# VectorE's score arrays hold three banks in place of two: wider shift passes in an attention and convolution kernel

## The chip, the cores and the metric

One core of a Trainium2 chip (trn2) runs the whole kernel. The metric is the device time of an execution in microseconds (us). The kernel before takes 719.72 us, the median of three runs (719.65 to 720.16). The core's engines work side by side, each through its own list of instructions, and wait for one another by semaphores: TensorE (PE, matmuls; PEld is its loading of weights), VectorE (DVE), ScalarE (ACT), GpSimd (POOL) and SyncE (SP). DMAs are issued from SP, POOL and ACT.

## The reference

Two independent blocks, whose results stand side by side in the output:

```python
# A: attention, S = 2048, D = 512, 32 heads of 16
qkv = x @ wqkv
scores = einsum("bhqd,bhkd->bhqk", q, k) * 16 ** -0.5
o = einsum("bhqk,bhkd->bhqd", softmax(scores), v)
a = o.reshape(B, S, D) @ wo
# B: a short and a long causal convolution, gated
kv = (k convolved with the 4 taps of shift_k) * v
y  = (kv convolved with ssm_k over all 2048 steps) + kv * ssm_D
b = q * y
out = concatenate([a, b], axis=-1)
```

All inputs are bf16. Nearly all of the time goes to A: 32 heads of 2048 x 2048 scores, each of which needs an exponential.

## The kernel before

**How the work is tiled.** The scores are cut into 2048 blocks of 128 keys by 512 queries of one head (512 columns in each of 128 partitions, one bank of PSUM). 64 blocks that belong together, 16 key tiles by four heads, are a group; 32 groups follow one another. Four blocks whose heads lie in different row groups can be multiplied side by side by PE (`qk_mm`, L910).

**Two engines make the exponentials.** ACT takes two or three banks at once with its exponential (`emit_exp`, L935: 128x1024 or 128x1536) and writes bf16 into a ring PT of 13 places. DVE takes one block at a time and makes the exponential without a table, in `exp_on_dve`: an addition with a floor (L1019) writes the score, scaled so that the bit pattern of the 16-bit result, read as a number, is about its power of two. Three more copies of this pattern, shifted by added integers, correct it: PV multiplies the values by all four terms with different weights (the first with VA, three with the scaled copies VS). The copies are made by two "shift passes" over bf16 data in SBUF:
- the near pass (L1029) writes one shifted copy of the first term;
- the far pass (L1036) writes two more from the first two, so it is twice as wide, and goes into a second array.

The arrays are RST, `R_ARR` of them, each with room for two terms of a set of blocks. A set is opened in the first free array by its first block (`take_array`); it is shifted when it holds its two blocks, or earlier as it is when the planner marks it "alone" (a group is being closed, or DVE has nothing else). The array of the first two terms is given back when these terms are multiplied for all blocks and the far pass has read it; the array of the far terms when those are multiplied (`give_back`). `R_LIN` limits how many sets may have their first array out at a time, and `dve_block` hands DVE no new set while no array is free.

**What sets the order.** All instruction lists are written by a planner that runs as the kernel is built. It goes step by step (T), gives each engine a clock of its own (`pe.t`, `dve.t`, `act.t`) and adds a price per instruction. At each step it emits the scores for ACT, perhaps a block for DVE (`dve_block`), terms to multiply (`pv_step`, L1128), and pieces of the rest: projections, the convolution (L1379, with weights WR read back from DRAM in 256 loads of 528 KB), output products, and filler matmuls that keep PE busy in gaps (`warm_up`, L1584). Ready shift passes wait in a list `flow` and are put where DVE has room, behind anything that empties a PSUM bank (`urgent`). `pv_step` multiplies terms when all four row groups have one, up to three levels at a time, and closes a group when all of its blocks are out.

A table, `POLICY`, changes the planner's thresholds as blocks go by (its first numbers count blocks). A class `Tensor` models that PE gets its instructions in stretches of 256, by loads that stand behind other DMAs: `FETCH` and `LOADED` say when the next stretch lands, and `release` holds back loads of WR that would delay it.

**The price list of the shift passes**, by the number of banks, as the planner sees it (time on the engine, time behind what it waits for):

```python
V512 = (0.60, 0.726)
FOUR = {1: (0.2, 0.326), 2: (0.333, 0.459), 4: (0.6, 0.726)}
```

A set of n blocks pays `FOUR[n]` for the near and `FOUR[2 * n]` for the far pass.

Of the kernel before, what the change touches and what calls it, by code (L numbers as in the profile page):

```python
# [88 lines left out]
N_TAIL = 9  # L89
MOST_OP = 3  # L90
OVER_OP = 0.1
R_ARR = 8
R_LIN = 5
LIN_D = 0.3
EVEN = 0.85
MOST_D = 3
# [52 lines left out]
WAIT = 3.0  # L149
LATE = 0.3  # L150
V512 = (0.60, 0.726)
FOUR = {1: (0.2, 0.326), 2: (0.333, 0.459), 4: (0.6, 0.726)}
TWO = {1: (0.333, 0.459), 2: (0.6, 0.726)}
SAME = 0.012
SWITCH = 0.105
# [3 lines left out]
BLOCK = 256  # L159
WORD0 = 65  # L160
FETCH = 3.3
SPAN = 6.0
QUIET = 6.0
LOADED = 1.6
WR_KB = 330
NEED = 10.0
FILL = 0.054


POLICY = (  # L170
    (0, {"DELAY": 3, "EVEN_MORE": 4, "FIRST": 2, "HALF": 0.35, "HURRY": 2, "JOIN": 0.15, "JOIN_D": 0.5, "LAGS": 16, "LATE": 0.3, "LATE_D": 0.4, "LEAD": 2, "LIN_D": 0.3, "LOW": 6.0, "LOW_2": 2.0, "LOW_A": 9.0, "LOW_L": 0.0, "MARGIN": 0.35, "MARGIN_D": 0.1, "MARGIN_P": 0.1, "MIN_L": 1, "NOW": 10, "OPEN": 40, "OVER_C": 0.1, "PRESS": 0, "PRIOR": 1, "R_LIN": 5, "SAFE": 1.0, "SOON": 0.3, "SOON_P": -0.1, "S_FX": 0.55, "TURN": 0.0}),
    (0, {"OVER_C": 0.05, "MIN_L": 2, "LIN_D": 0.0, "SAFE": 2.0}),
    (65, {"DELAY": 2, "JOIN": 0.25}),
    (194, {"LOW_2": 3.0}),
    (256, {"JOIN_D": 0.6, "EVEN_MORE": 6, "MARGIN_P": -0.3}),
    (320, {"LOW_2": 2.0, "JOIN_D": 0.5, "OVER_C": 0.1, "DELAY": 3, "EVEN_MORE": 4, "JOIN": 0.15, "MARGIN_P": 0.1, "MIN_L": 1, "LIN_D": 0.3, "SAFE": 1.0}),
    (384, {"JOIN": 0.25}),
    (448, {"PRESS": 20, "NOW": 6, "LOW": 5.5}),
    (514, {"MARGIN_P": 0.0, "OPEN": 30}),
    (578, {"LOW_2": 3.0, "PRESS": 0, "JOIN": 0.05, "MARGIN_P": 0.1, "NOW": 10, "OPEN": 40, "LOW": 6.0}),  # L180
    (640, {"PRIOR": 0, "HALF": 0.5}),
    (704, {"LOW_A": 2, "FIRST": 1}),
    (769, {"LOW_A": 9.0, "LOW_2": 2.0, "MARGIN": 0.32, "FIRST": 2, "PRIOR": 1, "JOIN": 0.15, "LEAD": 6}),
    (834, {"MARGIN": 0.35, "SOON_P": 0.1, "TURN": 0.2, "HALF": 0.35, "LEAD": 2, "SAFE": 2.0}),
    (899, {"LOW_2": 3.0, "LOW_L": 1, "MARGIN": 0.3, "R_LIN": 6, "SOON_P": -0.1, "TURN": 0.0, "SAFE": 1.0}),
    (961, {"HURRY": 0}),
    (1025, {"PRESS": 10}),
    (1090, {"LOW_2": 2.0, "LOW_L": 0.0, "LAGS": 10, "R_LIN": 5, "PRESS": 0, "HURRY": 2}),
    (1154, {"OVER_C": 0.0, "JOIN": 0.25}),
    (1218, {"MARGIN": 0.35, "OVER_C": 0.1, "LAGS": 8, "EVEN_MORE": 2, "JOIN": 0.15}),  # L190
    (1282, {"LOW_A": 5, "MARGIN_D": 0.0}),
    (1344, {"OVER_C": 0.15, "FIRST": 3, "LOW": 4.5, "SAFE": 2.0}),
    (1408, {"SOON": 0.2}),
    (1473, {"JOIN_D": 0.4, "OVER_C": 0.0}),
    (1537, {"JOIN": 0.05}),
    (1600, {"LOW_A": 2, "JOIN_D": 0.5, "MARGIN_D": 0.2, "OVER_C": 0.1, "LAGS": 16, "FIRST": 2, "EVEN_MORE": 4, "S_FX": 0.45, "JOIN": 0.15, "SOON": 0.3, "LOW": 6.0, "SAFE": 1.0}),
    (1665, {"JOIN_D": 0.7, "MARGIN": 0.3, "S_FX": 0.5, "LIN_D": 0.0}),
    (1729, {"LOW_A": 9.0, "JOIN_D": 0.5, "MARGIN_D": 0.1, "MARGIN": 0.35, "SOON_P": -0.2, "S_FX": 0.55, "LATE": 0.2, "TURN": 0.2, "LEAD": 6, "LIN_D": 0.3}),
    (1794, {"LAGS": 8, "DELAY": 4}),
    (1858, {"HURRY": 6, "JOIN": 0.05}),  # L200
    (1922, {"LAGS": 16, "HURRY": 2, "DELAY": 3, "SOON_P": -0.1, "LATE": 0.3, "JOIN": 0.15, "TURN": 0.0, "LEAD": 2, "LATE_D": 0.5}),
    (1985, {"LATE_D": 0.4}),
)


# [73 lines left out]
class Tensor(Eng):  # L279
# [32 lines left out]
    stalls = []  # L312

    def fetch(self, cross):
        end = max([b for a, b in self.loads[-12:] if a <= cross + 0.4], default=0.0)
        return max(cross + FETCH, end + LOADED)

    def spare(self):
# [15 lines left out]
def bass_concat_heads__mha_block__ssm_conv_h3__prompt_kernel(  # L334
# [25 lines left out]
    def sb(name, shape, dt=BF16):  # L360
# [24 lines left out]
    IDN = sb("IDN", [128, 128])  # L385
    IDP = sb("IDP", [128, 128])
    SHK = sb("SHK", [128, 4, 4])
    RST = sb("RST", [128, R_ARR, 2, 2, QB])
    VS = sb("VS", [128, 3, KT // 2, VROW])
    ZW = sb("ZW", [128, 32])  # L390
    JNK = sb("JNK", [128, 2], FP32)
# [12 lines left out]
    DG = OTF[:, 12 * QB + 2 * LEFT:16 * QB + 2 * LEFT].rearrange("p (c m d) -> p c m d", c=4, m=4)  # L404
    KZN = [OTF[:, 4 * QB:4 * QB + 2 * S].rearrange("p (c s) -> p c s", c=2),
           QNF[:, 0:2 * S].rearrange("p (c s) -> p c s", c=2)]
    XN = RST[:, R_ARR - 1, 0, :, :]
    PS = enter(nc.psum_tensor("PS", [128, 8, 512], FP32))


# [552 lines left out]
    def dve_block(T, n_act, aside=True):  # L963
        if T < T_DVE or aside and busy() or len(queue) < LAST_BLKS + 3 * TAIL_GAP + 4:
            return None
        if aside and conv_wants(T) and (state["go"] or conv_due() < T - PRESS):
            return None
        if aside and side[0] == "d" and (near(T, CLOSE) if T >= N_OPEN else early and early[0][0] <= T + 1):
            return None
        j = len(pairs) - 1  # L970
        j += not pairs or len(pairs[j]["h"]) == 2 or pairs[j]["alone"]
        if j == len(pairs) and (not arr_free or len([st for st in pairs[-8:] if 0 not in st["gone"]]) >= R_LIN or at(*arr_free[first_array()]) > pe.t + LIN_D):
            return None
        if todo() > BACKLOG:
            return None
        def pick_row(of, most):
            mine = [b for b in of if sub(b) == sub(of[0])][:most + EVEN_MORE]
            mine = [b for b in mine if even(b)]
            if not mine:
                return None  # L980
            there = [blk(b)[2] for b in on_dve if sub(b) == sub(of[0])]
            return min(mine, key=lambda b: there.count(blk(b)[2]))
        x = sub(queue[min(n_act, len(queue) - 1)])
        left = len([b for b in queue if sub(b) == x])
        if ends() + SAFE <= act.t + RATE * (left - n_act) + 1.3:
            return pick_row(queue, LOOK) if sub(queue[0]) == x else pick_row(queue[n_act:], 4)
        if x == subs[-1]:
            return None
        x = subs[subs.index(x) + 1]
        ahead = [b for b in queue if sub(b) == x]  # L990
        if len(ahead) < size[x] - AHEAD + 1 or x[0] not in h_q or (OF[x[0]], 0) not in h_k:
            return None
        return pick_row(ahead, 4)
# [11 lines left out]

    def give_back(st):
        for i in range(2):
            if i not in st["gone"] and min(st["n"][2 * i:2 * i + 2]) == len(st["h"]) and (len(st["h"]) == 2 or st["alone"]) and st["s"][1] is not None:
                st["gone"].add(i)
                arr_free[st["a"][i]] = (max(st["pv"][2 * i:2 * i + 2], key=lambda h: h[1]),) + ((st["s"][1],) if i == 0 else ())  # L1010

    def exp_on_dve(b, bank, h):
        if not pairs or len(pairs[-1]["h"]) == 2 or pairs[-1]["alone"]:
            a, dep = take_array()
            pairs.append({"h": [], "b": [], "alone": False, "a": [a, None], "s": [None, None], "dep": dep, "n": [0] * 4, "pv": [None] * 4, "gone": set()})
        j, half, st = len(pairs) - 1, len(pairs[-1]["h"]), pairs[-1]
# [6 lines left out]
        n = half + 1  # L1023

        def both(x, i0, i1):
            return x[:, i0:i1, 0:n, :].rearrange("p b a n -> p (b a n)") if n == 2 else x[:, i0:i1, 0, :]

        def near(us):
            st["s"][0] = dve.op(lambda e: e.tensor_scalar(both(lin, 1, 2).bitcast(U16), both(lin, 0, 1).bitcast(U16), SHIFTS[0], None, ALU.add),  # L1029
# [7 lines left out]
                                [st["h"][-1], st["s"][0], *dep], us=us)  # L1037
            give_back(st)

        begin = lambda: n == 2 or st["alone"]  # L1040
        if half == 0:
            st["f"] = [[]]
            flow.extend(st["f"])
# [117 lines left out]
    def pv_step(T):  # L1161
# [6 lines left out]
        for x in sorted({sub(b) for b in acts + dves}):  # L1168
# [7 lines left out]
            close = all(i in chunk_of for i in own) and T >= max(chunk_of[i] for i in own) + 2  # L1176
            if close and T < max(chunk_of[i] for i in own) + 2 + DELAY and n < NL and not any(p in pt_used for p in pt_next()):
                for b in d:
                    if len(pairs[on_dve[b][0]]["h"]) < MANY:
                        pairs[on_dve[b][0]]["alone"] = True  # L1180
                close = all(all_terms(b) is not None and at(all_terms(b)) <= pe.t + SOON_P for b in d)
            if close:
                for b in d:
                    while all_terms(b) is None:
                        k = dve.n
                        if len(pairs[on_dve[b][0]]["h"]) == 1:
                            pairs[on_dve[b][0]]["alone"] = True
                        if pick() is None:
                            early = next(y for y in d if all_terms(y) is not None and y in dves)
                            emit_pv([[(early, t)] for t in list(terms[early])], T)  # L1190
                            continue
                        advance(pick()[0] + MORE + 0.01)
                        assert dve.n > k
# [162 lines left out]
    def load_qn(i, deps):  # L1356
        for x in range(2):
            c0 = 256 * i + 128 * x
            h_qn[i] = dma(pool, d_q[0], QN[64 * x:64 * x + 64, :, :], q2[:, c0:c0 + 128].rearrange("(b i) d -> i b d", i=64),
                          deps if x == 0 else (), kb=930)  # L1360

    def conv_place(qd, g, rows):
        dst = PS[32 * g:32 * g + rows, BGB, :]
# [269 lines left out]
    while T < end[0] + 3:  # L1633
# [12 lines left out]
        advance(pe.t)  # L1646
        if LATE_D:
            late_block(T)
        if pairs and len(pairs[-1]["h"]) == 1 and not pairs[-1]["alone"] and dve.t < pe.t - ALONE and pick() is None:
            pairs[-1]["alone"] = True  # L1650
            advance(pe.t)
        emit_bg(T)
# [77 lines left out]
```

## Time and profile before

| | us |
|---|---|
| median of three runs | 719.72 |
| the profiled execution | 722.91 |
| its span | 721.1 |
| ACT busy | 703.4 (98%) |
| DVE busy | 691.3 (96%) |
| PE busy | 683.2 (95%) |
| POOL busy | 96.5 (13%) |

The profile shows one execution: from the span to the execution's own time there are 1.8 us outside of what is recorded. A group's row names its line, engine and operation, output and input with their shapes, its count, its busy time in all and the mean duration of one in ns; then the time its engine was idle just before, and the engine and line that ended most of it. Durations of neighbours on one engine can overlap, so the distance between two starts is shorter than a duration. The chain is the work that ended last, followed back from the end. PE's granted clock is given in shares of full speed.

### The profile page before, as it was taken

The numbers are of one execution on the slowest core, as the hardware profiler recorded it, in microseconds if no ns is written. First come the engines' busy times: TensorE is split into PE (matmuls) and PEld (weight loads), VectorE is DVE, ScalarE is ACT, GpSimd is POOL, SyncE is SP. The second block draws the span as 40 slices with busy tenths as digits, with TensorE's granted clock in tenths as the row PEclk, the third lists the DMA queues.
The fourth block names the chain that finished last, engine by engine and source line by source line (L and its number), as shares of the span: only waits on it lengthen the run. The fifth ranks groups of instructions, "written<-read, shape, count | busy, mean of one in ns | idle before, by whom it ended". The sixth has DMA issues, their size and how long they took to land.

```text
span 721.1 us, 25543 instructions
## 1 busy us (share of the span) xinstructions
PE 683.2 (95%) x11264; PEld 275.0 (38%) x11264; DVE 691.3 (96%) x1313; ACT 703.4 (98%) x646; POOL 96.5 (13%) x161
## 2 busy tenths in 40 slices
PE   9999999999899999999999999999999999999988
PEld 4334334334334434434333334333333333332244
DVE  5999999999799999999999999999999999999994
ACT  7999999999799999999999999999999999999997
POOL 5200311020020201002041020100202030211001
PEclk9999999999899999999999999999999999999999
DMA  9988644778857877588987578988885874713001
GB/s 229 289 215 270 141 168 140 258 254 299 269 204 277 292 269 264 161 306 294 332 258 217 184 247 313 338 288 307 295 318 189 310 281 163 288 57 59 16 17 32
DMA packets 83045, 164.23 MB, mean 228 GB/s; under 512 B 41232, under 2 KB 47256, under 8 KB 82680
## 3 DMA queue, kind: packets, MB, share of 16 engines
q1 hardware_dynamic: 75880, 153.61, 62.4%
q0 software_dynamic: 5856, 8.66, 4.9%
q8 instruction: 90, 1.47, 0.8%
q10 hardware_dynamic: 1200, 0.33, 0.2%
q14 instruction: 19, 0.16, 0.1%
HBM read 149.17 MB, written 8.54 MB: 219 GB/s over the span
## 4 chain that ended last, share of the span: by engine, by line
ACT 49%; DVE 32%; PE 18%; issue 1%
ACT PT L935 49%; DVE RST L1019 15%; DVE RST L1036 7%; PE PS L1128 7%; PE PS L910 6%; DVE RST L1029 4%; PE PS L1379 2%; DVE YB L1395 1%; DVE DT L1220 1%; PE PS L1294 1%; DVE KV L651 1%; PE PS L583 1%; DVE VA L666 1%; DVE KTo L640 1%; DVE VS L1060 0%
## 5 line engine op out<-in xcount | busy, mean ns | idle before, releaser
L935 ACT ACTIVATE PT<-PS 128x1024 bf16<-128x1024 f32 (+1 forms) x640 | 700.5, 1266 | 8.7 <-PE PS L910 7.8
L1019 DVE TENSOR_SCALAR RST<-PS 128x512 uint16<-128x512 f32 x513 | 342.6, 679 | 4.7 <-PE PS L910 4.0
L910 PE MATMUL PS<-QT,KTo 32*128 32x512 bf16 (+2 forms) x2248 | 257.6, 365 | 30.6 <-ACT PT L935 8.4
L1128 PE MATMUL PS<-PT,VA 128*32 128x512 bf16 (+2 forms) x1696 | 279.9, 367 | 0.3 <-issue 0.2
L1128 PE MATMUL PS<-RST,VS 128*32 128x512 bf16 (+1 forms) x1656 | 242.2, 370 | 0.3
L1036 DVE TENSOR_SCALAR RST<-RST 128x2048 uint16<-128x2048 uint16 x257 | 173.9, 681 | 0.6
L910 PEld LDWEIGHTS PS<-QT,KTo 32*128 32x128 bf16 x2248 | 67.9, 91 | 215.8 <-ACT PT L935 131.9
L1128 PE MATMUL PS<-RST,VA 128*32 128x512 bf16 (+1 forms) x552 | 123.7, 372 | 0.9 <-DVE DT L1220 0.7
L429 POOL DMA_DIRECT2D QT<-QS x120 | 65.6, 555 | 432.5 <-DVE QS L631 390.5
L1029 DVE TENSOR_SCALAR RST<-RST 128x1024 uint16<-128x1024 uint16 x257 | 101.6, 415 | 0.6
L1128 PEld LDWEIGHTS PS<-PT,VA 128*32 128x32 bf16 x1696 | 68.9, 94 | 79.4 <-issue 57.1
L1379 PE MATMUL PS<-WR,KV 128*28 128x128 bf16 (+7 forms) x4096 | 99.1, 221 | 0.0
L1379 PEld LDWEIGHTS PS<-WR,KV 128*30 128x30 bf16 (+7 forms) x4096 | 77.4, 101 | 27.9 <-issue 7.4
L1128 PEld LDWEIGHTS PS<-RST,VS 128*32 128x32 bf16 x1656 | 59.1, 95 | 53.6 <-issue 31.3
L1584 PE MATMUL PS<-IDN,ZW 128*32 128x256 bf16 (+3 forms) x150 | 37.9, 301 | 0.2
L1128 PEld LDWEIGHTS PS<-RST,VA 128*32 128x32 bf16 x552 | 30.8, 95 | 14.2 <-issue 7.2
L1220 DVE STREAM_TRANSPOSE DT<-PS 128x512 f32<-128x512 f32 x31 | 22.0, 709 | 3.8 <-PE PS L1128 3.5
L1395 DVE CAST YB<-PS 128x512 bf16<-128x512 f32 x32 | 21.8, 680 | 1.4 <-PE PS L1379 0.8
L429 POOL DMA_DIRECT2D out_dram<-OUTA x15 | 11.4, 759 | 62.5 <-DVE OUTA L1302 62.5
L1294 PE MATMUL PS<-WKV,OTN 128*128 128x512 bf16 (+1 forms) x68 | 18.9, 371 | 0.3 <-DVE OTN L1269 0.3
L615 PE MATMUL PS<-WKV,xT 128*128 128x128 bf16 x256 | 18.6, 220 | 0.5 <-DVE KTo L640 0.4
L592 PE MATMUL PS<-xT,WKV 128*128 128x512 bf16 (+1 forms) x64 | 16.7, 376 | 0.4
(72 smaller groups left out, 252.1 us busy)
## 6 DMA issues: line engine op xcount, KB each, us to landing
WR<-kz_scratch SPq DMA_DIRECT2D x256, 528.0 KB, 6.2
kz_scratch<-WR SPq DMA_DIRECT2D x4, 544.0 KB, 4.7
kt_scratch<-in_B_k_dram SPq DMA_DIRECT2D x1, 2048.0 KB
QN<-in_B_q_dram POOLq DMA_DIRECT2D x4, 512.0 KB, 7.0
out_dram<-QN POOLq DMA_DIRECT2D x4, 512.0 KB, 6.9
QT<-QS POOLq DMA_DIRECT2D x120, 16.0 KB, 3.4
out_dram<-OUTA POOLq DMA_DIRECT2D x15, 128.0 KB, 2.2
QN<-in_B_ssm_k_dram SPq DMA_DIRECT2D x1, 1024.0 KB, 8.2
```

Source lines behind the costliest of these rows:

```text
L429: f(outp, inp).then_inc(dsem.sem, 16)
L910: ins = e.matmul(PS[:, bank, i * w:i * w + w], lhsT=KTo[32 * s:32 * s + 32, OF[n_] % 2, kt * 128:(kt + 1) * 128], rhs=QT[32 * s:32 * s + 3 ...
L935: h_exp[T] = act.op(lambda e: e.activation(PT[:, p0:p0 + n, :].rearrange("p b f -> p (b f)"), PS[:, banks[0]:banks[0] + n, :].rearrange("p ...
L1019: st["h"].append(urgent(lambda e: e.tensor_scalar(lin[:, 0, half, :].bitcast(U16), PS[:, bank, :], FIX_ADD, FIX_HI, ALU.add, ALU.min), [h, ...
L1029: st["s"][0] = dve.op(lambda e: e.tensor_scalar(both(lin, 1, 2).bitcast(U16), both(lin, 0, 1).bitcast(U16), SHIFTS[0], None, ALU.add), [st ...
L1036: st["s"][1] = dve.op(lambda e: e.tensor_scalar(both(dst, 0, 2).bitcast(U16), both(lin, 0, 2).bitcast(U16), SHIFTS[1], None, ALU.add), [st ...
L1128: ins = e.matmul(dst, lhsT=w, rhs=rhs, start=first, stop=last, tile_position=(0, 32 * s))
L1220: h_t = urgent(lambda e: e.transpose(out=dt, in_=PS[:, PVB, :]), [h, h_mul.get(n - 1)], slack=S_T, us=(0.63, 0.751))
L1294: ins = e.matmul(PS[:, b, c0:c1], lhsT=OTN[:, PAIRS.index((o, qb)), t * 128:(t + 1) * 128], rhs=WO[:, o, c0:c1], start=(o == 0), stop=(o = ...
L1379: ins = e.matmul(dst, lhsT=KV[:, channel(qd) // 4, 2 * n:2 * NB, g], rhs=WR[:, (2 * qd + g // 2) % (R_W), w0:w0 + 128], start=(n == 0), st ...
L1395: bank_free[BGB] = h_ybw[0] = urgent(lambda e: e.tensor_copy(YB[:, qd % 8 // 4, :], src), [h, h_yb[0]], slack=S_C, us=V512)
L1584: pe.op(lambda e, s=s, dst=dst, rhs=rhs, rows=rows, first=first: e.matmul(dst, lhsT=ZW[:, 0:rows], rhs=rhs, start=first, stop=first, tile_ ...
```

## The change

The arrays hold `SET = 3` banks for each of their two terms. So the shift passes of a full set cover 1536 columns (near) and 3072 columns (far), where they covered 1024 and 2048. There are five arrays of three in place of eight of two, and at most four sets with their first array out, where there were five. A set counts as complete with three blocks, and a group's closing marks a set of one or two blocks as alone. The price list becomes a formula that gives the old prices for 1, 2 and 4 banks and extends them to 8. `both`, which makes the pass's operand, joins the banks into one run of columns where they lie side by side: for a full set, or where only one of the two terms is taken.

In the same step the planner's beliefs on loads change (LOADED, ISSUED, SPAN, and the 512 KB loads of q, `load_qn`, are booked at 1400 KB in place of 930), and the table POLICY is another: other thresholds, at other blocks, so that the order of the work is new all along the kernel.

```diff
-R_ARR = 8
-R_LIN = 5
+SET = 3
+R_ARR = 5
+R_LIN = 4
-FOUR = {1: (0.2, 0.326), 2: (0.333, 0.459), 4: (0.6, 0.726)}
+FOUR = {n: (0.067 + 0.1333 * n, 0.193 + 0.1333 * n) for n in range(1, 9)}
-SPAN = 6.0
+SPAN = 6.5
-LOADED = 1.6
+LOADED = 2.4
+ISSUED = 1.1
 POLICY = (
...
     def fetch(self, cross):
-        end = max([b for a, b in self.loads[-12:] if a <= cross + 0.4], default=0.0)
+        end = max([b for a, b in self.loads[-12:] if a <= cross + ISSUED], default=0.0)
         return max(cross + FETCH, end + LOADED)
...
-    RST = sb("RST", [128, R_ARR, 2, 2, QB])
+    RST = sb("RST", [128, R_ARR, 2, SET, QB])
...
-        j += not pairs or len(pairs[j]["h"]) == 2 or pairs[j]["alone"]
+        j += not pairs or len(pairs[j]["h"]) == SET or pairs[j]["alone"]
...
         def both(x, i0, i1):
-            return x[:, i0:i1, 0:n, :].rearrange("p b a n -> p (b a n)") if n == 2 else x[:, i0:i1, 0, :]
+            return x[:, i0:i1, 0:n, :].rearrange("p b a n -> p (b a n)") if n == SET or i1 - i0 == 1 else x[:, i0:i1, 0:n, :]
...
-        begin = lambda: n == 2 or st["alone"]
+        begin = lambda: n == SET or st["alone"]
...
-                    if len(pairs[on_dve[b][0]]["h"]) < MANY:
+                    if len(pairs[on_dve[b][0]]["h"]) < SET:
                         pairs[on_dve[b][0]]["alone"] = True
...
-                        if len(pairs[on_dve[b][0]]["h"]) == 1:
+                        if len(pairs[on_dve[b][0]]["h"]) < SET:
                             pairs[on_dve[b][0]]["alone"] = True
...
-                          deps if x == 0 else (), kb=930)
+                          deps if x == 0 else (), kb=1400)
...
-        if pairs and len(pairs[-1]["h"]) == 1 and not pairs[-1]["alone"] and dve.t < pe.t - ALONE and pick() is None:
+        if pairs and len(pairs[-1]["h"]) < SET and not pairs[-1]["alone"] and dve.t < pe.t - ALONE and pick() is None:
             pairs[-1]["alone"] = True
```

More of the change, by code (lines that the diff above doesn't have):

```diff
@@ L170 @@
 POLICY = (
-    (0, {"DELAY": 3, "EVEN_MORE": 4, "FIRST": 2, "HALF": 0.35, "HURRY": 2, "JOIN": 0.15, "JOIN_D": 0.5, "LAGS": 16, "LATE": 0.3, "LATE_D": 0.4, "LEAD": 2, "LIN_D": 0.3, "LOW": 6.0, "LOW_2": 2.0, "LOW_A": 9.0, "LOW_L": 0.0, "MARGIN": 0.35, "MARGIN_D": 0.1, "MARGIN_P": 0.1, "MIN_L": 1, "NOW": 10, "OPEN": 40, "OVER_C": 0.1, "PRESS": 0, "PRIOR": 1, "R_LIN": 5, "SAFE": 1.0, "SOON": 0.3, "SOON_P": -0.1, "S_FX": 0.55, "TURN": 0.0}),
-    (0, {"OVER_C": 0.05, "MIN_L": 2, "LIN_D": 0.0, "SAFE": 2.0}),
@@ L173 @@
[L173 to L202, printed above, removed]
+    (0, {"DELAY": 3, "EVEN_MORE": 4, "HURRY": 2, "JOIN": 0.15, "JOIN_D": 0.5, "LAGS": 16, "LATE": 0.3, "LATE_D": 0.4, "LEAD": 2, "LOW_2": 2.0, "LOW_A": 9.0, "LOW_L": 0.0, "MARGIN_D": 0.1, "MARGIN_P": 0.1, "MIN_L": 1, "NEED": 10.0, "NOW": 10, "OVER_C": 0.1, "PRESS": 0, "PV_ON": 3, "PV_WANT": 3, "SOON": 0.3, "SOON_P": -0.1, "S_FX": 0.55, "TURN": 0.0, "YIELD": -4}),
@@ new lines @@
+    (64, {"S_FX": 0.45, "MARGIN_P": -0.3, "LEAD": 6}),
+    (128, {"PV_WANT": 1, "S_FX": 0.55, "MARGIN_P": 0.1, "LEAD": 2}),
+    (257, {"PV_WANT": 3, "PRESS": 10, "YIELD": -8, "HURRY": 0}),
+    (323, {"LOW_2": 3.0}),
+    (384, {"LOW_L": 2, "HURRY": 2}),
+    (449, {"PRESS": 20}),
+    (512, {"LOW_2": 2.0, "LOW_L": 0.0, "PRESS": 0, "YIELD": -4}),
+    (704, {"LAGS": 12}),
+    (769, {"MARGIN_D": 0.0, "EVEN_MORE": 6}),
+    (833, {"SOON_P": -0.2, "EVEN_MORE": 2, "S_FX": 0.5, "MIN_L": 2}),
+    (896, {"MARGIN_D": 0.1, "LAGS": 16, "SOON_P": -0.1, "EVEN_MORE": 4, "S_FX": 0.55, "MIN_L": 1, "SOON": 0.2}),
@@ new lines @@
+    (960, {"OVER_C": 0.0}),
+    (1024, {"OVER_C": 0.1, "SOON": 0.3}),
+    (1154, {"LOW_2": 1.8, "DELAY": 2, "LATE_D": 0.3, "SOON": 0.4}),
+    (1216, {"JOIN_D": 0.4, "LATE": 0.2, "NOW": 6}),
+    (1281, {"S_FX": 0.5, "JOIN": 0.25, "LATE_D": 0.4}),
+    (1345, {"LOW_2": 2.0, "JOIN_D": 0.5, "DELAY": 3, "S_FX": 0.55, "LATE": 0.3, "JOIN": 0.15, "SOON": 0.3, "NOW": 10}),
+    (1408, {"OVER_C": 0.0}),
+    (1474, {"JOIN": 0.05}),
+    (1538, {"OVER_C": 0.1, "LATE": 0.2, "JOIN": 0.15}),
+    (1665, {"LEAD": 6}),
@@ L203 @@
+    (1729, {"PV_ON": 0, "YIELD": 0}),
+    (1795, {"JOIN": 0.25}),
+    (1856, {"PV_ON": 3, "YIELD": -4, "LATE": 0.3, "JOIN": 0.15, "LEAD": 2}),
+    (1921, {"LOW_2": 1.5, "NEED": 12.0}),
+    (1985, {"LOW_A": 3, "LAGS": 12, "TURN": 0.1}),
 )
@@ L406, in bass_concat_heads__mha_block__ssm_conv_h3__prompt_kernel @@
            QNF[:, 0:2 * S].rearrange("p (c s) -> p c s", c=2)]
-    XN = RST[:, R_ARR - 1, 0, :, :]
+    XN = RST[:, R_ARR - 1, 0, 0:2, :]
     PS = enter(nc.psum_tensor("PS", [128, 8, 512], FP32))
@@ L1007, in give_back @@
         for i in range(2):
-            if i not in st["gone"] and min(st["n"][2 * i:2 * i + 2]) == len(st["h"]) and (len(st["h"]) == 2 or st["alone"]) and st["s"][1] is not None:
+            if i not in st["gone"] and min(st["n"][2 * i:2 * i + 2]) == len(st["h"]) and (len(st["h"]) == SET or st["alone"]) and st["s"][1] is not None:
                 st["gone"].add(i)
@@ L1012, in exp_on_dve @@
     def exp_on_dve(b, bank, h):
-        if not pairs or len(pairs[-1]["h"]) == 2 or pairs[-1]["alone"]:
+        if not pairs or len(pairs[-1]["h"]) == SET or pairs[-1]["alone"]:
             a, dep = take_array()
```

## The prediction

> **What bounds the kernel now.** I read the page's busy shares first, then its chain, then the groups by form, then the stretches at both ends and at the one dip.
>
> ```profile
> span 721.1 us, 25543 instructions
> ...
> PE 683.2 (95%) x11264; PEld 275.0 (38%) x11264; DVE 691.3 (96%) x1313; ACT 703.4 (98%) x646; POOL 96.5 (13%) x161
> ...
> ACT 49%; DVE 32%; PE 18%; issue 1%
> ```
>
> Three engines are nearly full. The chain changes hands between ScalarE (ACT), VectorE (DVE) and TensorE (PE), because the exponentials are shared out between ACT and DVE: whichever gets time back can take blocks from the other. Is PE a third bound, or only busy?
>
> ```profile
> L935 ACT ACTIVATE PT<-PS 128x1024 bf16<-128x1024 f32 (+1 forms) x640 | 700.5, 1266 | 8.7 <-PE PS L910 7.8
> L1019 DVE TENSOR_SCALAR RST<-PS 128x512 uint16<-128x512 f32 x513 | 342.6, 679 | 4.7 <-PE PS L910 4.0
> L1036 DVE TENSOR_SCALAR RST<-RST 128x2048 uint16<-128x2048 uint16 x257 | 173.9, 681 | 0.6
> L1029 DVE TENSOR_SCALAR RST<-RST 128x1024 uint16<-128x1024 uint16 x257 | 101.6, 415 | 0.6
> L1584 PE MATMUL PS<-IDN,ZW 128*32 128x256 bf16 (+3 forms) x150 | 37.9, 301 | 0.2
> ```
>
> PE spends 37.9 us on L1584, which only fills gaps to keep its clock, so PE has that much to give. ACT waits 8.7 us and the exponentials on DVE 4.7 us in all. The 2048 blocks of scores stand as 513 on DVE, hence 1535 in ACT's 640 instructions. Where do ACT and DVE stand idle?
>
> ```profile
> 0.00:20.00 20.00, 18.05 (x158) 7.71 (x158) 11.23 (x28) 15.10 (x16) 9.38 (x17) 1.00 0.99 248
> 180.00:200.00 20.00, 18.06 (x279) 7.17 (x276) 15.01 (x29) 16.10 (x15) 0.00 (x0) 0.83 0.84 282
> 700.00:720.00 20.00, 17.02 (x430) 9.69 (x421) 10.31 (x28) 15.84 (x16) 2.01 (x3) 1.00 0.09 29
> ```
>
> (Columns: stretch, its length, PE, PEld, DVE, ACT, POOL, granted clock, DMA share, GB/s.) Of DVE's 29.8 idle us, 8.8 lie at the start, 9.7 at the end and 5.0 in the dip at 180 to 200, so 6.3 in all the rest. DVE is full wherever it may work: time saved there is usable.
>
> **Prices.** How long does an instruction hold DVE or ACT? Durations overlap their neighbours, so I take the distance between starts, from the chain and, for the shift pass, the timeline:
>
> ```profile
> 46.06 1.80 DVE RST L1019 x3
> 106.37 47.31 ACT PT L935 x43
> ```
> ```profile
> 404.42 0.75 DVE L1029 TENSOR_SCALAR RST<-RST 128x1024 uint16<-128x1024 uint16 x2
> ```
>
> Three L1019 in 1.80 us are 0.600 us each, 0.079 below the 0.679 duration. The two near passes from 404.42 end after 0.75 us, so they start 0.75 - 0.415 = 0.335 apart, again 0.08 less than the duration. A far pass of 2048 then holds DVE for 0.681 - 0.079 = 0.602. The two widths give the slope, (681 - 415)/1024 = 0.260 ns a column, and a fixed part of 0.336 - 1024 x 0.260/1000 = 0.070 us an instruction. ACT's long run is 47.31/43 = 1.10 us an instruction; over the whole kernel 700.5/1535 = 0.456 us a block.
>
> **The change part by part.**
>
> Wider passes. A near pass of 1536 costs 0.070 + 0.400 = 0.470, a far pass of 3072 costs 0.070 + 0.799 = 0.869: 1.339 a set of three, 0.446 a block. Now it is 0.336 + 0.602 = 0.938 a set of two, 0.469 a block. The columns stay the same, only instructions go: 513 blocks make 171 sets in place of 257, so 86 x 2 x 0.070 = 12.0 us of DVE go. Neither width is in the trace. Bounds: nothing saved if the slope were worse beyond 2048 columns; 12.0 if the line holds, which I take, as two widths lie on it and the new ones are at most 1.5 times away.
>
> Sets that do not fill. A group's closing, or an idle DVE, makes the planner shift a set as it is. Now all sets but one are full (257 passes, 513 blocks). With three to gather, each of the 31 group changes may leave one more broken set: at most 31 x 0.140 = 4.3 us, at least 0. I take the middle, 2.2, which leaves 12.0 - 2.2 = 9.8 us.
>
> Sharing it. DVE's saving shortens the run only by taking blocks from ACT. A block costs DVE 0.600 + 0.446 = 1.046 and frees 0.456 on ACT, so x us off ACT cost DVE 2.29x, and DVE too must end x earlier: 9.8 = 3.29x, **x = 3.0 us**, 6.5 blocks moved. With all 12.0 it is 3.6; with an ACT that loses only half of the gain to idling, 1.5. This is the term that decides: 12 us of work buy about 3.
>
> PE's price for it. A block on DVE has four terms to multiply in place of one.
>
> ```profile
> 185.60 0.39 PE L1128 MATMUL PS<-RST,VS 128*32 128x512 bf16 x3
> 185.82 0.39 PE L1128 MATMUL PS<-PT,VA 128*32 128x512 bf16 x4
> ```
>
> Four row groups run side by side at 0.22 us a level, so 6.5 x 3 / 4 x 0.22 = 1.1 us more. I cost it at nothing, since L1584's 37.9 us are the cover; without it the gain would be 1.9.
>
> Longer passes ahead of evictions. PE waits for DVE to empty banks, and a far pass holds DVE 0.27 us longer:
>
> ```profile
> PEld PS L910 <- ACT PT L935: 131.9, 324, 0.9
> PEld PS L910 <- DVE RST L1019: 31.4, 75, 1.3
> ACT PT L935 <- PE PS L910: 7.8, 18, 1.9
> ```
>
> (Totals, times, longest.) Behind the 75 waits, 0.27 each would be 20 us of PE's waiting, but PE mostly waits for ACT, 131.9 us, and ACT waited for PE only 18 times. Between 0 and 20/3.29 = 6 us; I take 0, nearest to ACT's row, and keep the 6 for the rival below.
>
> Five arrays of three for eight of two: 15 places for 16, but lent in larger lots. How many are in use? Counts of exponentials, near passes, far passes and multiplications of terms (DVE L1019, L1029, L1036; PE on RST), from the start:
>
> ```profile
> 0.00:350.00 350.00, 163.29 (x245) 0.99 0.75 244
> 0.00:550.00 550.00, 264.41 (x397) 0.99 0.77 254
> ```
> ```profile
> 0.00:350.00 350.00, 47.62 (x120) 0.99 0.75 244
> 0.00:550.00 550.00, 77.85 (x196) 0.99 0.77 254
> ```
> ```profile
> 0.00:350.00 350.00, 81.01 (x120) 0.99 0.75 244
> 0.00:550.00 550.00, 132.46 (x196) 0.99 0.77 254
> ```
> ```profile
> 0.00:350.00 350.00, 127.96 (x965) 0.99 0.75 244
> 0.00:550.00 550.00, 209.72 (x1571) 0.99 0.77 254
> ```
>
> At 350 us 245 - 240 = 5 blocks wait for their shifts, and all 245 + 240 + 480 = 965 terms so far made are used. At 550 us 5 blocks wait, and 2 of 1573 terms. So the stock lies ahead of the shifts, about five blocks: three arrays of two now, two of three then, and three stay for far terms and the next set. It fits, with less over. I cost it at 0; the bound is in the rival.
>
> The table, the limit of open sets (5 to 4) and the planner's beliefs on loads (LOADED 1.6 to 2.4, ISSUED 0.4 to 1.1, SPAN 6.0 to 6.5, the 512 KB load of q at 1400 for 930) add no instruction; they place work. What they may touch is the dip:
>
> ```profile
> 187.22 1.78 issue
> ```
> ```profile
> 186.00:188.00 2.00, 1.22 (x25) 0.43 (x21) 1.55 (x4) 1.69 (x2) 0.00 (x0) 1.00 0.34 67
> 188.00:190.00 2.00, 1.00 (x9) 0.30 (x13) 0.00 (x0) 0.36 (x1) 0.00 (x0) 0.68 0.86 192
> 190.00:192.00 2.00, 2.00 (x44) 1.30 (x36) 1.09 (x2) 1.09 (x1) 0.00 (x0) 0.50 0.81 239
> ```
>
> PE stood 1.78 us with no releaser, which I read as late instructions behind loads; afterwards its granted clock was 0.50. ACT lost 20 - 16.10 = 3.9 us here, half of its waiting. If the stricter beliefs keep such a stall away, up to 3.9 us go; if a new order brings another, as much comes. I take 0, as one row supports both signs. The Trainium skill (TensorE: Matmul & The Clock Gate, the two states) has the clock halve after an idle window of about 3.4 us. By that rule a stall of 1.78 us alone would leave the clock be, and the dip would be worth about 1.8 us and not 3.9; the row shows the halved clock after it, so I stay with the row.
>
> **The sum.** The profiled execution took 722.91 us, 721.1 of it span; the median of the runs is 719.72, 3.2 less, so the dip may be smaller in them. The chain's 3.0 us, with 0 for the rest, make the profiled execution 719.9 and the median **716.7 us**. The likeliest case's own range is 715.0 to 718.2 (gains of 4.7, 3.6 and a load better placed, down to 1.5).
>
> **The rivals.**
>
> (1) The dip goes as well: 716.7 - 3.9 = 712.8. For it: LOADED and ISSUED now count a load issued up to 1.1 us after PE begins a new stretch of instructions. Against: the runs without profile are 3.2 us faster already, so the dip may be the profiled execution's own.
>
> (2) Arrays run short, slower. With five arrays, a set whose terms wait for their row holds two of them, and a new set can't begin: DVE idles. Each idle us costs 1/3.29 = 0.30 us, so from 9.8 us idle, 1.4% of the span, the change is slower. At 4%, 29 us, it is (29 - 9.8) x 0.30 = 5.8 us slower: **725.5**. For it: the third block comes 550/397 = 1.39 us after the second, and every first block waits for it; two sets in work leave a single array. Against it: the stock of five blocks above. The 6 us of later evictions would show at the same place, as PE waiting for L1019.
>
> (3) The saving is taken up by broken sets and by terms that come 1.39 + 0.40 us later at each group's end: DVE is less busy, the block shares stay, within 0.2%: 719.7.
>
> (4) The wide passes run at half rate. Slope 0.520: a set of three costs 2 x 0.070 + 4608 x 0.520/1000 = 2.54 us, 171 x 2.54 - 257 x 0.938 = 193 us more DVE, 193/3.29 = 59 us slower, 778. In the code a full set is one unbroken run of 1536 or 3072 columns, as the runs of 1024 and 2048 are now, so I give it 1%. The Trainium skill (VectorE: DVE Perf Modes, What auto-detection actually checks) takes the fast mode away where the outermost dimensions are odd and unequal. By that rule the full sets keep it, as do sets of two, whose far pass has an outermost dimension of two; the trace agrees with four columns a cycle at 0.260 ns, and no run here shows an odd one.
>
> **How the numbers follow.** Likeliest case 0.45; dip gone too 0.15; arrays short 0.28; taken up 0.11; half rate 0.01. A difference of 0.2%, 1.4 us, is about what a measurement of this kernel can tell from no change. Faster: 0.45 + 0.15, less 0.02 of the likeliest that falls short of 1.4 us, 0.58. Same: 0.11 + 0.02, less 0.03 of (3) that slips below, 0.10. Slower: 0.28 + 0.01 + 0.03 = 0.32. The range goes down to rival (1), 712.8, and up to 724.0, which leaves out the far half of (2), some 0.13, case (4), and 0.05 at the bottom.
>
> **What would show it.** Near passes of 1536 columns at about 548 ns and far passes of 3072 at about 948 ns, 171 to 185 of each; some 520 exponentials in L1019's place and 1528 blocks on ACT; DVE still without idle time between 20 and 700 us. Wrong if: passes are slower than the line (rate), L1019's count falls below 510 with DVE idle (arrays), the count of passes is above 200 (broken sets), or a stretch with an issue wait and a clock of 0.5 is there or not there (the dip).

## The result

The changed kernel takes **727.98 us** (median of four runs, 727.64 to 728.36), against 719.94 for the kernel before beside it: a ratio of 1.0115, with a 95% interval of 1.0095 to 1.0135. Forecast were 716.7 us, in a range from 712.8 to 724.0. It is 8.0 us slower where 3.0 less were expected.

The page of the changed kernel, its busy shares, its chain and the groups that answer to those of before:

```profile
span 725.9 us, 25440 instructions
...
PE 683.8 (94%) x11299; PEld 276.5 (38%) x11299; DVE 681.3 (94%) x1129; ACT 706.2 (97%) x647; POOL 98.2 (14%) x161
...
ACT 68%; PE 22%; DVE 8%; issue 1%
...
L932 ACT ACTIVATE PT<-PS 128x1024 bf16<-128x1024 f32 (+1 forms) x641 | 703.2, 1273 | 6.6 <-PE PS L907 5.6
L1016 DVE TENSOR_SCALAR RST<-PS 128x512 uint16<-128x512 f32 x505 | 337.6, 681 | 13.7 <-PE PS L907 11.7
...
L1033 DVE TENSOR_SCALAR RST<-RST 128x3072 uint16<-128x3072 uint16 (+1 forms) x169 | 160.2, 948 | 1.6
...
L1026 DVE TENSOR_SCALAR RST<-RST 128x1536 uint16<-128x1536 uint16 (+1 forms) x169 | 92.5, 550 | 2.3
L1581 PE MATMUL PS<-IDN,ZW 128*32 128x512 bf16 (+3 forms) x200 | 43.7, 293 | 0.0
```

(All lines stand three earlier than before: L1016 is the old L1019.) The wide passes are there and cost what was expected, 948 and 550 ns, in 169 sets. But DVE made 505 exponentials, 8 fewer than before, and not 520. It was idle 13.7 us ahead of them, 11.7 of that waiting for scores, and its share of the chain fell from 32% to 8% while ACT's rose from 49% to 68%. DVE has got its time back and stands with it. How much, away from both ends, shows the stretch from 20 to 700 us, first before, then after (PE, PEld, DVE, ACT, POOL, clock, DMA share, GB/s):

```profile
20.00:700.00 680.00, 648.16 (x10685) 257.57 (x10685) 669.73 (x1259) 672.48 (x616) 85.14 (x141) 0.99 0.69 233
```
```profile
20.00:700.00 680.00, 646.74 (x10651) 256.45 (x10650) 657.72 (x1073) 675.03 (x617) 86.77 (x141) 1.00 0.70 233
```

DVE's idle time is 680 less its busy time: 10.3 us before, of which the dip at 187 us holds 5.0, and 22.3 after. The dip itself is gone (granted clock 1.00).

A second part of the loss lies at the very end. The last store of an output tile by POOL and the store of the last product by ACT, on the timeline, before and after:

```profile
713.52 0.54 POOL L429 DMA_DIRECT2D out_dram<-OUTA  x1 [2.36 <-DVE OUTA L1302]
718.68 0.37 ACTq L429 DMA_DIRECT2D out_dram<-QT  x1
```
```profile
719.50 0.54 POOL L426 DMA_DIRECT2D out_dram<-OUTA  x1 [4.29 <-DVE OUTA L1299]
720.17 0.37 ACTq L426 DMA_DIRECT2D out_dram<-QT  x1
```

Before, the span ends 721.1 - 718.68 = 2.4 us after the last product's store; after, 725.9 - 720.17 = 5.7. So 3.3 of the 8.0 us come behind all computing, and some 4.7 are left to the work itself. (In the profiles the last product's store is only 1.5 us later, because the profiled execution of the kernel before, with its dip, was 3.0 us longer than the median.) The last section returns to this.

### The profile page after: what moved, and what is told of

Read it like the earlier page. It is cut to its first block, busy times and chain, and to the rows that moved or that the text cites. A ratio compares the mean times of both kernels' runs of the same rounds, so it can differ in the third digit from the quotient of the medians.

```text
span 725.9 us, 25440 instructions
## 1 busy us (share of the span) xinstructions
PE 683.8 (94%) x11299; PEld 276.5 (38%) x11299; DVE 681.3 (94%) x1129; ACT 706.2 (97%) x647; POOL 98.2 (14%) x161
## 4 chain that ended last, share of the span: by engine, by line
ACT 68%; PE 22%; DVE 8%; issue 1%
ACT PT L932 68%; PE PS L1125 8%; PE PS L907 6%; DVE RST L1016 4%; PE PS L1291 2%; DVE RST L1033 2%; PE PS L1376 1%; PE PS L601 1%; DVE RST L1026 1%; PE PS L580 1%; DVE YB L1392 1%; PE PS L589 1%; PE PS L720 1%; PE PS L1403 0%; PE PS L612 0%
## 5 line engine op out<-in xcount | busy, mean ns | idle before, releaser
L932 ACT ACTIVATE PT<-PS 128x1024 bf16<-128x1024 f32 (+1 forms) x641 | 703.2, 1273 | 6.6 <-PE PS L907 5.6
L1016 DVE TENSOR_SCALAR RST<-PS 128x512 uint16<-128x512 f32 x505 | 337.6, 681 | 13.7 <-PE PS L907 11.7
L1125 PE MATMUL PS<-PT,VA 128*32 128x512 bf16 (+2 forms) x1701 | 276.4, 366 | 0.5 <-DVE VA L663 0.5
L1125 PE MATMUL PS<-RST,VS 128*32 128x512 bf16 (+1 forms) x1641 | 236.4, 368 | 0.3 <-issue 0.3
L1033 DVE TENSOR_SCALAR RST<-RST 128x3072 uint16<-128x3072 uint16 (+1 forms) x169 | 160.2, 948 | 1.6
L1125 PE MATMUL PS<-RST,VA 128*32 128x512 bf16 (+1 forms) x547 | 127.8, 368 | 2.9 <-DVE DT L1217 2.7
L426 POOL DMA_DIRECT2D QT<-QS x120 | 68.6, 580 | 450.1 <-DVE QS L628 412.1
L1376 PE MATMUL PS<-WR,KV 128*32 128x128 bf16 (+7 forms) x4096 | 95.4, 220 | 0.0
L1026 DVE TENSOR_SCALAR RST<-RST 128x1536 uint16<-128x1536 uint16 (+1 forms) x169 | 92.5, 550 | 2.3
L1581 PE MATMUL PS<-IDN,ZW 128*32 128x512 bf16 (+3 forms) x200 | 43.7, 293 | 0.0
L1581 PEld LDWEIGHTS PS<-IDN,ZW 128*32 128x32 bf16 x200 | 17.4, 96 | 12.0 <-issue 2.7
```

Source lines behind the costliest of these rows:

```text
L426: f(outp, inp).then_inc(dsem.sem, 16)
L932: h_exp[T] = act.op(lambda e: e.activation(PT[:, p0:p0 + n, :].rearrange("p b f -> p (b f)"), PS[:, banks[0]:banks[0] + n, :].rearrange("p ...
L1016: st["h"].append(urgent(lambda e: e.tensor_scalar(lin[:, 0, half, :].bitcast(U16), PS[:, bank, :], FIX_ADD, FIX_HI, ALU.add, ALU.min), [h, ...
L1033: st["s"][1] = dve.op(lambda e: e.tensor_scalar(both(dst, 0, 2).bitcast(U16), both(lin, 0, 2).bitcast(U16), SHIFTS[1], None, ALU.add), [st ...
L1125: ins = e.matmul(dst, lhsT=w, rhs=rhs, start=first, stop=last, tile_position=(0, 32 * s))
L1376: ins = e.matmul(dst, lhsT=KV[:, channel(qd) // 4, 2 * n:2 * NB, g], rhs=WR[:, (2 * qd + g // 2) % (R_W), w0:w0 + 128], start=(n == 0), st ...
```

## The experiments

Three theories. **Gathering**: the passes wait for a third block, so terms come late and in lumps, and DVE stands without ready work. **Arrays**: five arrays of three are too few, whatever the widths. **Table**: the other order and the other beliefs on loads are to blame. The order of the work is sensitive to its thresholds, so the kernels compared share a table. One entry differs: the limit of open sets, `R_LIN`, which stands in the table's first row too, is 5 with sets of two and 4 with sets of three, split ones included. No run changes this limit alone, so whatever it costs is counted with the arrays below. All runs are edits of the changed kernel. In the tables "last product" is the start of ACT's last store, which leaves out what happens behind it; "DVE idle" is that of 20 to 700 us in the profiled execution.

### A table of one row: sets, gathering, arrays

Sets of two and of three, as in the kernels before and after, with the old beliefs:

```diff
-SET = 3
-R_ARR = 5
-R_LIN = 4
+SET = 2
+R_ARR = 8
+R_LIN = 5
-SPAN = 6.5
-LOADED = 2.4
-ISSUED = 1.1
+SPAN = 6.0
+LOADED = 1.6
+ISSUED = 0.4
-                          deps if x == 0 else (), kb=1400)
+                          deps if x == 0 else (), kb=930)
 POLICY = (
...
```

The sets of three have the same edit without its first six lines, and 4 for `R_LIN` in the table. In the third kernel (split), two blocks are shifted as soon as there are two, and the third by itself, into the same arrays of three; each half of a set keeps handles of its own:

```diff
-        n = half + 1
+        cuts = (2, 3)
+        lo = max([c for c in (0, *cuts) if c <= half])
+        hi = half + 1
+        n = hi - lo
...
-        begin = lambda: n == SET or st["alone"]
-        if half == 0:
+        begin = lambda: hi in cuts or st["alone"]
+        if half == lo:
             st["f"] = [[]]
```

In the fourth (gather), sets of two, a full set waits until the next one is opened:

```diff
-        begin = lambda: n == SET or st["alone"]
+        begin = lambda: n == SET and len(pairs) > j + 1 or st["alone"]
```

A group's closing and an idle DVE release the waiting set by marking it alone.

> Sets of two, eight arrays, the old beliefs on loads, and a table of one row (the same for this run and the next three) in place of the searched one. It is the base for the three others. What the searched table is worth isn't known: between 0 and 15 us, so 720 to 735 us. Theory 'table' (the new table and beliefs are a worse order, the wide sets cost nothing): the three-block run of the same table comes out 0 to 3 us faster than this. Theories 'gathering' and 'arrays': it comes out 6 to 10 us slower than this.

> Sets of three, five arrays, the old beliefs and the same one-row table. 'Table': 0 to 3 us faster than the sets of two with this table. 'Gathering' (passes wait for a third block, terms come late and in lumps, DVE stands without ready work and ACT takes the blocks) and 'arrays' (five arrays are too few): 6 to 10 us slower, with some 500 blocks on DVE and DVE waiting for scores (L907's line) more than 10 us.

> As the sets of three with five arrays, but the passes don't wait for the third block: two blocks are shifted together, the third by itself, into the same arrays of three. Arrays as in the change, two instructions more a set: 170 x 2 x 0.070 = 24 us more for DVE. 'Gathering': 4 to 8 us faster than the sets of three, in spite of that. 'Arrays': no faster, and up to 24 / 3.29 = 7 us slower.

> Sets of two in eight arrays with passes of the old widths, but a full set waits for the next set's first exponential before it is shifted (unless a group closes or DVE has nothing else). No pass is added or widened. 'Gathering': 3 to 6 us slower than the sets of two with this table, as waiting alone costs. 'Arrays' and 'table': within 1.5 us of it, as arrays are not short with eight.

| one-row table | median us | last product | blocks on DVE | DVE idle |
|---|---|---|---|---|
| sets of two, eight arrays | 727.99 | 723.3 | 510 | 14.9 |
| sets of three, five arrays | 736.99 | 731.0 | 501 | 34.6 |
| split | 733.31 | 729.4 | 508 | 10.6 |
| gather | 731.68 | 726.2 | 512 | 11.9 |

The sets of three lose 9.0 us. Splitting their passes wins back 3.7, a little under the least expected, with more work for DVE; 1.5 of that lie ahead of the last product's store, and 2.0 behind it, where the span goes on for 4.3 us with sets of three and for 2.4 with split ones. (Both profiled executions had a low clock for a while: 0.62 on the mean of 172 to 174 us with split sets, and 0.62 on the mean of 716 to 720 us with sets of three.) Waiting alone costs sets of two 3.7, of which 2.9 lie ahead of that store. So gathering costs time by itself, and it isn't all. The groups show what it does; first the sets of three, then the split ones:

```profile
L990 DVE TENSOR_SCALAR RST<-PS 128x512 uint16<-128x512 f32 x501 | 335.8, 682 | 22.1 <-PE PS L881 20.3
L1007 DVE TENSOR_SCALAR RST<-RST 128x3072 uint16<-128x3072 uint16 x168 | 159.2, 948 | 2.1 <-PE PS L1099 0.8
L1000 DVE TENSOR_SCALAR RST<-RST 128x1536 uint16<-128x1536 uint16 x168 | 92.2, 550 | 2.5
```
```profile
L990 DVE TENSOR_SCALAR RST<-PS 128x512 uint16<-128x512 f32 x508 | 342.3, 680 | 6.7 <-PE PS L881 5.5
L1012 DVE TENSOR_SCALAR RST<-RST 128x2048 uint16<-128x2048 uint16 x339 | 184.5, 550 | 1.3 <-PE PS L1105 0.7
L1003 DVE TENSOR_SCALAR RST<-RST 128x1024 uint16<-128x1024 uint16 x339 | 111.9, 353 | 0.9
```

The split passes take 296.4 us of DVE for 251.4, yet the kernel is faster and DVE takes 7 blocks more: its wait for scores falls from 20.3 to 5.5 us. The passes that are ready are what DVE does between two banks of scores. While a set waits for its third block there is none. The trace of the changed kernel shows it; one such wait on its timeline:

```profile
292.46 0.56 DVE L1026 TENSOR_SCALAR RST<-RST 128x1536 uint16<-128x1536 uint16 x1
292.93 0.68 DVE L1016 TENSOR_SCALAR RST<-PS 128x512 uint16<-128x512 f32 x1
293.53 0.95 DVE L1033 TENSOR_SCALAR RST<-RST 128x3072 uint16<-128x3072 uint16 x1
294.40 0.68 DVE L1016 TENSOR_SCALAR RST<-PS 128x512 uint16<-128x512 f32 x1
295.70 0.69 DVE L1016 TENSOR_SCALAR RST<-PS 128x512 uint16<-128x512 f32 x1 [0.62 <-PE PS L907]
```

The full set is shifted, two blocks of the next are made, and for 0.62 us DVE has neither scores nor a pass. Counted along the timeline from 20 to 700 us, the changed kernel has 27 waits of over 0.1 us ahead of an exponential, 11.3 us in all. In 20 of them, 8.9 us, just two blocks stood unshifted and no far pass was due: the set waited for its third block, which goes into an array already out, so no lack of arrays held it back. In the one-row kernel with sets of three it is 17.8 of 20.2 us; in the kernel before, the waits ahead of exponentials were 2.6 us in all, and for only 0.5 us of them was no pass ready.

Splitting also makes the passes shorter, which could let PE have its banks back sooner. With one row it did not: PE's wait for L990, 29.3 us with sets of three, is 31.5 with split ones. (With the random table below it falls from 35.1 to 27.2, so there a part may come from this.)

Waiting in sets of two does something else. DVE stays full there, but ACT's wait for PE, in the order two and gather, grows:

```profile
ACT PT L906 <- PE PS L881: 9.0, 26, 0.9
```
```profile
ACT PT L906 <- PE PS L881: 11.7, 31, 1.8
```

With the random table below it goes from 11.3 to 17.4. The terms come later, and PE, which multiplies them in its own order, is later with scores. That the one follows from the other was not tested by itself. A set that waits also keeps its array longer; but where arrays are short for sets of two (below), DVE makes 504 or 505 blocks and is idle for over 19 us, and neither is seen here.

### The same with a random table

The four kernels again, with another table, the same in each: 18 rows behind the one row. (The forecast speaks of 31 rows; the kernels hold these 19.) Five of the 18 set only values that hold already, so this table is a near relative of the first one and not an independent one.

```diff
 POLICY = (
     (one row)
+    (18 rows, thresholds drawn at random)
```

> The four kernels of the one-row table again, with another table (31 rows drawn at random from the values that the two searched tables use, the same rows in all four): sets of two, eight arrays. An order is sensitive to its table, so a difference seen with one table may be luck. As the base: 722 to 734 us.

> Sets of three, five arrays, the random table. 'Gathering' and 'arrays': 5 to 11 us slower than the sets of two with this table (it was 9.0 with one row). 'Luck of a table': the difference changes its sign or falls below 2 us.

> Sets of three, five arrays, two blocks and then the third shifted apart, the random table. 'Gathering': 2 to 7 us faster than the sets of three (it was 3.7 with one row), with DVE's wait for scores (L881) below 10 us. 'Arrays': no faster. 'Luck of a table': either way.

> Sets of two that wait for the next set's first exponential, the random table. 'Gathering': 2 to 8 us slower than the sets of two (it was 3.7 with one row). 'Arrays' and 'luck of a table': within 2 us, or faster.

| random table | median us | last product | blocks on DVE | DVE idle |
|---|---|---|---|---|
| sets of two, eight arrays | 728.74 | 723.9 | 514 | 10.2 |
| sets of three, five arrays | 740.70 | 732.8 | 506 | 30.3 |
| split | 732.97 | 726.9 | 509 | 10.4 |
| gather | 736.81 | 730.8 | 516 | 12.1 |

Every sign is the same: 12.0 slower with three (its two times are 4.2 us apart), 7.7 won back by splitting, 8.1 lost by waiting. Each lies a little above the range expected for gathering (to 11, 7 and 8). DVE's idle time between 20 and 700 us is the steadiest sign in these eight kernels: 30 us and more where three are gathered, 10 to 15 elsewhere.

### The arrays and the beliefs

Sets of two with six arrays; sets of three with six, for which one row of the ring WR gives its room; and the random table with the changed beliefs on loads.

```diff
-R_ARR = 8
+R_ARR = 6
```
```diff
-R_ARR = 5
-R_W = 9
+R_ARR = 6
+R_W = 8
```

> Sets of two with six arrays in place of eight (12 places for 16; three sets at work), one-row table, old beliefs. Five arrays of three hold two and a half sets. 'Arrays' as the larger part of the loss: 6 to 10 us slower than the sets of two with eight arrays (728.0). 'Gathering' as the larger part: 1 to 5 us slower.

> Sets of three with six arrays (18 places), one-row table, old beliefs. The sixth array takes the room of one row of the ring WR of convolution weights, which has eight rows for nine. 'Arrays' as the larger part: 4 to 8 us faster than with five (737.0). 'Gathering': between 2 us faster and 2 us slower.

> Sets of two, eight arrays, the random table of the second four runs, but the changed beliefs on loads (LOADED 2.4, ISSUED 1.1, SPAN 6.5, loads of q at 1400). If the beliefs carry a part of the loss: 2 to 5 us slower than with the old ones (728.7), as loads are held back for nothing. If they don't: within 2 us, or faster by what PE stood waiting for its instructions.

> Sets of three, five arrays, the random table, the changed beliefs on loads. If the beliefs carry a part of the loss: 2 to 8 us slower than with the old ones (740.7). If they don't: within 2 us, or faster.

Six arrays of two took 738.71 us, 10.7 more than eight and above both forecasts (6 to 10 if arrays are the larger part, 1 to 5 if gathering is). DVE was idle for 19.3 us there and made 505 blocks, so idle time and fewer blocks come with short arrays too. Six arrays of three took 737.94, 0.9 more than five, and its two times lie 4.8 us apart; the longer one is the profiled one, whose clock was 0.50 from 720 to 728 us. The beliefs took 729.41 and 741.30, 0.7 and 0.6 more than the old ones: they carry no part of the loss. So few arrays do hurt sets of two, and more arrays seemed not to help sets of three. Four more runs: the ring's control, split sets with five and with six arrays on the same short ring, and six arrays of two with the random table. Their edits are those above, combined.

> The control for six arrays of three: sets of three, five arrays, eight rows of WR, one-row table, old beliefs. If the ring's ninth row is worth nothing: within 2 us of 737.0. If six arrays helped and the ring's loss hid it: 4 us or more above 737.9.

> Two blocks and the third shifted apart, five arrays of three, eight rows of WR, one-row table. Base of the next run. Within 2 us of the 733.3 with nine rows if the ring's ninth row is worth nothing.

> The same with six arrays of three (18 places). If too few arrays are what is left of the loss once the passes don't gather (5.3 us in 733.3 against 728.0): 3 to 6 us faster than with five arrays and the same ring. If it is the price of the added passes (10 us of DVE more than sets of two, 3 us of time): within 2 us.

> Sets of two with six arrays, the random table. If the 10.7 us of the one-row table were the arrays: 7 to 13 us slower than with eight (728.7). If a part was luck of that order: 1 to 6 us slower.

| eight rows of WR, one-row table | five arrays | six arrays |
|---|---|---|
| gathered by three | 739.31 | 737.94 |
| split | 735.43 | 730.37 |

The short ring itself costs a little over 2 us (739.31 for 736.99, 735.43 for 733.31), so the ninth row is worth something. With split passes the sixth array wins 5.1 us, of which 1.7 lie ahead of the last product's store (727.1 against 725.4). With gathered ones it wins 1.4, less than the spread of its runs. Six arrays of two with the random table took 734.20 us, 5.5 more than eight, so the size of this loss hangs on the order. Arrays are a second cause; the larger one in this table is the gathering: 3.9 us with five arrays, 7.6 with six. To the last product's store, splitting is worth 5.2 us with five arrays (732.3 to 727.1). The sixth array was tried with the limit of four open sets left as it was.

### A table searched alike for both

The table was made for its kernel, so both kinds of sets were given one from the same search of the same length.

> Sets of two, eight arrays, old beliefs, with a table searched as long and in the same way as the next run's (segment by segment of 64 blocks, 24 draws of one threshold each, a draw kept where the planner's own end comes earlier). 722 to 728 us, as the one-row table gave 728.0 and the searched table of the kernel before is at 720.

> Sets of three, five arrays, old beliefs, a table from the same search of the same length. If the table makes the sign (a searched order hides the gathering and the few arrays): within 2 us of the searched sets of two, or faster. If the sets and arrays do: 3 to 10 us slower than the searched sets of two, the same side as with the one-row table (9.0) and the random one (12.0).

They took 724.65 us (ratio to before 1.009, 1.006 to 1.012) and 729.44 (1.0141, 1.0113 to 1.017): 4.8 us more for sets of three, on the same side as the three other comparisons of the two kinds. Of this, 2.6 lie ahead of the last product's store (718.9 and 721.5) and the rest behind it. DVE's stretch, two, then three:

```profile
20.00:700.00 680.00, 641.43 (x10638) 256.85 (x10665) 669.56 (x1253) 673.40 (x615) 83.80 (x141) 1.00 0.70 233
```
```profile
20.00:700.00 680.00, 644.29 (x10539) 257.10 (x10570) 653.34 (x1066) 674.48 (x615) 85.18 (x140) 1.00 0.70 233
```

Its idle time is 10.4 and 26.7 us. A search narrows the distance, it doesn't turn it; both searched tables begin with the one row of the first comparison. None of these kernels beats the one before, whose own table is worth 727.99 - 720.41 = 7.6 us beside one row (720.41 is the kernel before in the same comparison), about as much as the whole change. The changed kernel's own table, with its beliefs, is worth as much to it, 736.99 - 727.98 = 9.0 us, so nothing here points to a worse table.

## Why the prediction was wrong

**Wider passes: right.** 948 and 550 ns for the forecast 948 and 548. The slope holds to 3072 columns, (948 - 681)/1024 = 0.261 ns. Rival (4) is out; the Trainium skill's rule on the outermost dimensions (VectorE: DVE Perf Modes, What auto-detection actually checks) keeps the fast mode for one unbroken run, and this trace agrees.

**Sets that do not fill: missed, and it hid the point.** I put 2.2 us on broken sets. One set of 169 broke. The planner doesn't break sets, it waits, and a wait is no instruction: it had no term in the sum.

**Sharing it: the step that failed.** "DVE is full wherever it may work: time saved there is usable" took a busy DVE for one whose time can be spent anywhere. What DVE can take is set by when banks of scores come, and between them it needs ready passes. Before, DVE hardly ever waited there without one (0.5 us). Fewer and wider passes that start later leave holes just there: 22.3 idle us for 10.3, or for 5.3 without the dip, with 8.9 us of waiting while a set lacked its third block, and 8 blocks fewer where 6.5 more were forecast. The idle time grew by 12.0 us, as much as the forecast had counted as saved, and the eight blocks came back to ACT (703.2 us busy for 700.5).

**Five arrays: costed at 0, in part wrong.** The counts at two instants were right, but five waiting blocks there say nothing of the moments when more are wanted. Two arrays fewer cost sets of two 10.7 and 5.5 us; a sixth array of three won 5.1 us once nothing gathers, only 1.7 of them ahead of the last product's store.

**The rivals.** Rival (2) had the side, its price (725.5) was 2.5 us short, and both of its marks came: L1016 below 510, and DVE idle. That the price came so near is in part luck: it took 29 us of idle time, where 12.0 came (17.0 without the dip), for which its formula gives only 0.7 to 2.2 us, and it had nothing for the 3.3 us at the end. The reason it names first, the arrays, was the smaller one in the one-row table. The reason it gives in passing, that the first block waits for the third, was the larger there, and it is what the waits in the changed kernel's trace show; it deserved a rival of its own: rival (3) had it as harmless at a group's end.

**PE's price: not put to the test; later evictions: right.** No block moved to DVE, so PE never had to pay for one. Filler matmuls took 43.7 us for 37.9, so it had the time; its wait for L1016 hardly moved (31.4 us before):

```profile
PEld PS L907 <- ACT PT L932: 132.7, 316, 1.2
PEld PS L907 <- DVE RST L1016: 34.0, 81, 1.1
```

**Beliefs and the dip.** The beliefs moved nothing under the random table (0.7 and 0.6 us). The dip is absent after, but it seems to have been mostly the profiled execution's own: that took 722.91 us where the median is 719.94, so little could be won there.

**What was left out.** The end of the kernel, 3.3 us, has no term in the prediction. The order of the last products was taken as given, though the change brings another table and with it another order.

How the 8.0 us divide between gathering and arrays in the changed kernel itself, with its own table, stays open: the parts were measured with other tables, where they ran from 4 to 8 us for gathering and from 1 to 5 for a sixth array of three. Each of these holds a part that lies behind the last product, and `R_LIN` was never varied alone.

## What to carry to other kernels

Merging instructions saves their fixed cost but makes the work wait for the last of its inputs; on an engine that fills its gaps with that very work, price the wait, not only the instructions. An engine that is 96% busy isn't one whose saved time can be spent: ask what it will do in each gap, and when that becomes ready. And where an order is searched, compare kinds of kernels under several shared tables, and look at a sign that doesn't hang on the order, as the waits of DVE with a set unfilled here.

## What the runs showed that I had not expected

A late store by POOL goes with a late end. In 19 of the 20 profiles the span ends 6.4 or 7.1 us after the start of POOL's last store of an output tile, wherever that was: in the changed kernel 725.9 - 719.50 = 6.4, and with sets of three and one row, whose span is 735.3 us and whose last store by POOL is this row of the timeline,

```profile
728.86 0.54 POOL L400 DMA_DIRECT2D out_dram<-OUTA  x1 [3.52 <-DVE OUTA L1273]
```

6.4 again. The one exception is the kernel before: POOL's last store is 5.2 us ahead of ACT's there, and the end comes 2.4 us after ACT's instead, as near as in any of them. In the changed kernel the data of POOL's last store lands 2.0 us after its issue (2.4 on the median of its last three), so the rest is spent behind the landing. The Trainium skill (DMA: Bandwidth & Descriptors, Issuing engine by pattern) gives simple stores to SyncE and calls that path generally faster; in the trace the last stores by ACT and SP, of 64 KB where POOL's are of 128, land in 1.7 and 1.8 us. That a store by SyncE in POOL's place would win the 3.3 us back was not tried.
